# Sequence product of an FNet-SwiGLU kernel: split right sides stored once and reloaded in the last two sets, and no split of the a21 block by itself

## The chip, the core and the metric

The kernel runs on one core of a Trainium2 chip. The metric is the device time of one execution in microseconds (us). The engines named below are PE (TensorE, the matrix multiplier), ACT (ScalarE), DVE (VectorE), POOL (GpSimd) and SP (SyncE). Every engine works through its own list of instructions in order. Transfers between HBM and the on-chip memory (SBUF) are issued by SP, which fills the queue that the profile calls q1, and by POOL, which fills q0. Both queues are served by the same 16 DMA engines.

## What is computed

```python
xn = layernorm(x)                                   # x: 2048 x 640
a, b = xn @ hid_re.T, xn @ hid_im.T                 # hid: 640 x 640
s = seq_re @ a - seq_im @ b                         # seq: 2048 x 2048
g = silu((silu(xn @ w_gate) * (xn @ w_up)) @ w_down)   # F = 1536
out = x + s * g
```

All of it is in 32-bit floats.

## The kernel before

**Numbers in two parts.** A matrix product of 32-bit floats is made of three matmuls on rounded operands. `split` (L184) turns an operand into a high part, a rounded copy made by ACT (L192), and a low part, the operand minus the high part, made by DVE (L197, or L199 with a factor). `mm3` (L210) multiplies high by high, high by low and low by high (L213, L214, L215) into one PSUM bank. A PSUM bank is 128 x 512; there are 8. Split operands live in an SBUF arena called `hl`, everything else in an arena called `raw`.

**Stages.** The program runs four *sets* of the sequence product (`seq(0)` to `seq(3)`), and then, twice, the hidden product (`hid`), the gate and up products (`gate_up`) and the down product (`down`).

**A set.** Set k multiplies blocks of the sequence matrix (real part for even k, imaginary for odd k; two of the four column chunks of 512 per set) by xn. It is a 2 x 2 block product in Strassen's manner: left blocks a11, a12, a21, a22 of the sequence matrix, right blocks b11 to b22 of xn, and seven products p1 to p7 in place of eight. The last 128 of the 640 columns of xn do not take part in this; their two halves, d1 and d2, are multiplied directly: a11 d1 + a12 d2 into bank 6, a21 d1 + a22 d2 into bank 7. Each left block comes in four pieces g = 0 to 3 of 128 x 1024 floats (512 KB). A piece is loaded by SP (L575, in `load`), or added onto a buffer in SBUF by an accumulating transfer that POOL issues (L580, in `accumulate`), or added by DVE (L583, in `add`). `operand` (L586) splits a piece, and `right_operand` (L592) splits the right side of a product, or the sum of right sides that it needs (`right`, L467). The right sides are the same in all four sets and are split again in each.

In set 0 the kernel opens with p1 of sets 0 and 1 side by side (`opening`, L668; the second one's result is put aside as `ahead["s1"]` and `ahead["d1"]`, copied out of PSUM by L241). Then comes a phase `d`, that splits a21 and multiplies it by d1 (L741), then p5 with the left side a21 + a22, which is made by accumulating a22 onto the same buffer after the split of a21, then p2, p6, p3, p7, p4. In the other sets the order is p1 (not in set 1), d, p2, p5, p6, p3, p7, p4. `down` uses the same order through `strassen` (L251).

**Later stages.** `down_operands` (L506) makes the split right sides of `down`, from w_down, and stores them to `d_dram`; `down` reloads them (L1021). It is a generator, and `gate_up` of the first half advances it twice for each of its middle ten column blocks.

**What sets the order.** All instructions are written into a `Plan` with a planned time on PE's clock, at 0.226 us for each matmul. `prod(lead, ...)` plans an instruction `lead` us before the product that needs it, `post(..., after=)` some us after the product that it follows. The instructions are sorted by planned time, and each engine's list is that order. `place` gives every buffer its offset in an arena from the planned lifetimes. On the chip nothing waits for the planned time: an instruction runs when its engine has done the one before it and its data and buffers are free.

Of the kernel before, what the change touches and what calls it, by code (L numbers as in the profile page):

```python
# [7 lines left out]
F32 = mybir.dt.float32  # L8
# [15 lines left out]
HL_KB, RAW_KB = 95, 111  # L24
# [113 lines left out]
def tile_fnet_swiglu(  # L138
# [112 lines left out]
    def strassen(tag, groups, get, top, dop, result, end=False):  # L251
# [73 lines left out]
        def a21(g):  # L325
            X[g] = get(21, g)
            return operand("d", g, X[g])

# [4 lines left out]
        def s_1(g):  # L333
            V[g] = get(22, g)
# [22 lines left out]
        phase("d", None, a21, (2, 1))  # L357
# [3 lines left out]
        phase("p5", b3, s_1)  # L361
# [15 lines left out]
        if not end:  # L377
            run("p4", ops["p4"], None, None, None, (2, 2))
# [4 lines left out]
        dw, dkeys = dop(2)  # L383
# [80 lines left out]
    p_dram = dram.tile([2, NC, ND, P, TC], F32, name="p_dram")  # L464
    sums = {}

    def right(p, g, lead):  # L467
# [6 lines left out]
        def new(what, a, b, op):  # L474
            if (what, g) not in sums:
                name = pl.buf((what, g), "raw", 1024)
                view = lambda a=0, n=4: raw(name).rearrange("p (a b) -> p a b", b=256)[:, a:a + n]
# [16 lines left out]
        if p == "p7":  # L494
# [4 lines left out]
            return a  # L499
        return quad(int(p[1]) - 1, 2, P)  # L500


    d_names = ("p1", "p2", "d1", "d2", "p3", "p5", "p6", "p7", "p4")
    d_dram = {(p, g): dram.tile([P, 768 if p[0] == "d" else 1536], F32, name=f"d_{p}_{g}") for g in range(2) for p in d_names}

    def down_operands():  # L506

        for g in range(2):
# [10 lines left out]
            for p in d_names:  # L519
                b11, b12, b21, b22 = (quad(*q) for q in ((0, 0), (0, 1), (1, 0), (1, 1)))  # L520
                made = {"p5": (b11, b12, ALU.subtract), "p6": (b11, b22, ALU.add),
                        "p7": (b12, b22, ALU.subtract), "p4": (b21, b11, ALU.subtract)}
# [32 lines left out]
    def seq(k):  # L555
# [36 lines left out]
        def right_operand(p, g, per):  # L592

            width = P if p[0] == "d" else 256
            sums, high, low = LEAD.get(("T" + p, per * g), LEAD.get("T" + p, LEAD["T"])) if fresh else LEAD["T"]
# [8 lines left out]
            for i in range(per):  # L604
                top[p, per * g + i] = name, sub, (sub + i) * width

# [4 lines left out]
        def run(*parts, order=None):  # L611
# [6 lines left out]
            for i, g in order or [(0, g) for g in range(4)]:  # L618
                p, left, banks, direct = parts[i]
# [3 lines left out]
                s = left(g)  # L623
                for kk in (2 * g, 2 * g + 1):
# [41 lines left out]
        Y, R = {}, {}  # L666

        def opening():  # L668
# [42 lines left out]
            for kk in range(8):  # L711
                for i, banks, db in part:
# [15 lines left out]
            evict(ahead["s1"], b1, after=1)  # L728
            evict(ahead["d1"], (b3[0],), after=1)
# [405 lines left out]
```

## Time and profile before

| | |
|---|---|
| time, median of 3 runs | 993.39 us (992.28 to 993.47) |
| profiled execution: its own time / its span | 993.8 us / 991.7 us |
| mean granted TensorE clock | 0.995 |
| PE busy | 979.3 us, 4300 matmuls |
| DVE busy / ACT busy / POOL busy | 717.2 / 497.8 / 106.4 us |
| bytes moved by DMA | 182.18 MB, mean 184 GB/s |

The span runs from the first to the last instruction; the execution's own time has 2.1 us more around it. A busy PE includes matmuls that overlap in its pipeline, so PE's time is read from the spacing of its matmuls. The view of windows gives, for a stretch of the span, the busy time of each engine with the number of instructions, the granted clock, the busy share of the 16 DMA engines and the rate in GB/s.

### The profile page before, as it was taken

The page shows a single profiled execution, that of the slowest core. Times are in us where ns is not written, and L with a number is a line of the kernel's source. Part 1 is how long each engine was busy: PE and PEld are TensorE (multiplying, and loading weights), DVE is VectorE, ACT ScalarE, POOL GpSimd, SP SyncE. Part 2 cuts the span into 40 slices and gives each one's busy share as a digit, 9 for nine tenths or more (in the row PEclk, how much of TensorE's full clock was granted, in tenths as well). Part 3 has the DMA queues.
Part 4 walks back from the last instruction along what each step waited for, and adds up shares of the span by engine and source line. Part 5 has one row for each costly group of instructions (what it writes and reads, how often), then busy time and mean ns, then how long its engine had stood idle before and what let it go on. Part 6 is the DMA issues. An engine that isn't in the chain of part 4 may idle for free.

```text
span 991.7 us, 11754 instructions
## 1 busy us (share of the span) xinstructions
PE 979.3 (99%) x4300; PEld 804.7 (81%) x4300; DVE 717.2 (72%) x942; ACT 497.8 (50%) x716; POOL 106.4 (11%) x175
## 2 busy tenths in 40 slices
PE   9989999999999999999999999999999999999998
PEld 5778888788888888888888888888888888888886
DVE  6889867965875595377678787687568666666685
ACT  5585652755455554424655555444334544445342
POOL 0380111011101010000111110000010100000000
PEclk9989999999999999999999999999999999999999
DMA  9788687575757493842645344679860211105683
GB/s 337 208 210 227 223 217 180 171 237 135 180 191 222 108 264 116 288 163 107 250 191 181 138 165 164 211 264 354 293 230 28 89 45 53 54 27 191 219 290 127
DMA packets 72185, 182.18 MB, mean 184 GB/s; under 512 B 6528, under 2 KB 22144, under 8 KB 72128
## 3 DMA queue, kind: packets, MB, share of 16 engines
q1 hardware_dynamic: 57792, 127.81, 38.0%
q0 software_dynamic: 14336, 53.63, 19.6%
q8 instruction: 33, 0.54, 0.2%
q14 instruction: 24, 0.20, 0.1%
HBM read 147.85 MB, written 33.57 MB: 183 GB/s over the span
## 4 chain that ended last, share of the span: by engine, by line
PE 91%; DMA 3%; DVE 2%; ACT 2%; issue 1%; SPq 0%; POOL 0%; DVEq 0%; ACTq 0%
PE ps L214 30%; PE ps L213 30%; PE ps L215 30%; DMA raw<-in_cs 3%; DVE hl L197 1%; ACT hl L192 1%; DMA p_dram<-raw 1%; ACT raw L454 0%; DVE raw L583 0%; DVE bst L421 0%; ACT raw L241 0%; POOL raw L580 0%; DVE raw L246 0%; SPq L686 0%; SPq L412 0%
## 5 line engine op out<-in xcount | busy, mean ns | idle before, releaser
L213 PE MATMUL ps<-hl 128*128 128x512 f32 (+1 forms) x1424 | 554.6, 389 | 5.3 <-ACT raw L241 5.3
L214 PE MATMUL ps<-hl 128*128 128x512 f32 (+1 forms) x1424 | 554.0, 389 | 0.1
L215 PE MATMUL ps<-hl 128*128 128x512 f32 (+1 forms) x1424 | 553.6, 389 | 0.0
L192 ACT ACTIVATE hl<-raw 128x1024 fp32r<-128x1024 f32 (+7 forms) x509 | 374.5, 782 | 284.4 <-PE ps L215 54.1
L197 DVE TENSOR_TENSOR hl<-raw,hl 128x1024 fp32r<-128x1024 f32 (+5 forms) x438 | 394.7, 931 | 121.8 <-ACT hl L192 76.9
L213 PEld LDWEIGHTS ps<-hl 128*128 128x128 f32 x1424 | 268.0, 188 | 62.5 <-ACT raw L241 6.1
L214 PEld LDWEIGHTS ps<-hl 128*128 128x128 f32 x1424 | 267.9, 188 | 56.2 <-DVE hl L197 0.7
L215 PEld LDWEIGHTS ps<-hl 128*128 128x128 f32 x1424 | 267.9, 188 | 55.2
L241 ACT ACTIVATE raw<-ps 128x512 f32<-128x512 f32 (+1 forms) x120 | 78.0, 670 | 106.6 <-PE ps L215 80.9
L246 DVE TENSOR_TENSOR raw<-ps,raw 128x512 f32<-128x512 f32 (+1 forms) x93 | 74.6, 803 | 54.1 <-PE ps L215 52.4
L1005 DVE TENSOR_TENSOR raw<-raw 128x512 f32<-128x512 f32 x24 | 16.6, 692 | 50.1 <-ACT raw L1004 50.0
L918 DVE TENSOR_TENSOR raw<-raw 128x256 f32<-128x256 f32 (+1 forms) x96 | 47.7, 518 | 0.0
L580 POOL DMA_DIRECT2D raw<-in_cs x36 | 32.3, 953 | 140.3 <-DVE raw L583 81.0
L199 DVE SCALAR_TENSOR_TENSOR hl<-raw,hl 128x384 fp32r<-128x384 f32 (+4 forms) x71 | 41.2, 580 | 7.3 <-PE ps L215 2.9
L583 DVE TENSOR_TENSOR raw<-raw 128x1024 f32<-128x1024 f32 x28 | 34.1, 1219 | 10.8 <-DMA raw<-in_cs 10.7
L1067 POOL DMA_DIRECT2D out<-raw x10 | 6.7, 671 | 302.1 <-DMA hl<-d_p 175.1
L657 POOL DMA_DIRECT2D p_dram<-raw x24 | 17.5, 772 | 198.1 <-DVE raw L246 163.4
L871 DVE TENSOR_TENSOR raw<-raw 128x1024 f32<-128x1024 f32 (+1 forms) x24 | 23.9, 1040 | 6.8 <-DMA raw<-in_xt 4.7
L983 ACT ACTIVATE raw<-raw 128x512 f32<-128x512 f32 x24 | 15.2, 632 | 22.1 <-DVE raw L246 22.1
L843 POOL DMA_DIRECT2D y_dram<-raw x20 | 10.8, 546 | 132.5 <-ACT raw L241 132.5
L1004 ACT ACTIVATE raw<-ps 128x512 f32<-128x512 f32 x24 | 14.3, 594 | 21.0 <-PE ps L215 21.0
L533 POOL DMA_DIRECT2D d_p<-hl x28 | 15.1, 541 | 79.7 <-ACT hl L192 65.6
(49 smaller groups left out, 191.6 us busy)
## 6 DMA issues: line engine op xcount, KB each, us to landing
raw<-in_cs SPq DMA_DIRECT2D x82, 512.0 KB, 6.1
hl<-d_p SPq DMA_DIRECT2D x56, 384.0 KB, 4.4
raw<-in_cs POOLq DMA_DIRECT2D x36, 512.0 KB, 8.9
raw<-in_wb SPq DMA_DIRECT2D x24, 640.0 KB, 4.5
d_p<-hl POOLq DMA_DIRECT2D x28, 384.0 KB, 2.9
raw<-p_dram SPq DMA_DIRECT2D x8, 1280.0 KB, 11.1
p_dram<-raw POOLq DMA_DIRECT2D x16, 512.0 KB, 7.5
raw<-in_hd SPq DMA_DIRECT2D x20, 320.0 KB, 8.1
```

The source lines that it names most:

```text
L192: nc.scalar.activation(like(hl(dst, 0, a, n)), src(), AF.Copy, scale=1.0 if scale is None else scale)
L197: nc.vector.tensor_tensor(lo, src(), hi, op=ALU.subtract)
L199: nc.vector.scalar_tensor_tensor(lo, src(), scale, hi, op0=ALU.mult, op1=ALU.subtract)
L213: nc.tensor.matmul(o, w(0), m(0), start=first, stop=False, skip_group_check=True)
L214: nc.tensor.matmul(o, w(0), m(1), start=False, stop=False, skip_group_check=True)
L215: nc.tensor.matmul(o, w(1), m(0), start=False, stop=True, skip_group_check=True)
L241: pl.post(lambda: nc.scalar.activation(wide(raw(dst, a, n)), pair(b), AF.Copy), pkeys(b), [(dst, a)], after)
L246: pl.post(lambda: nc.vector.tensor_tensor(wide(raw(dst, a, n)), pair(b), wide(raw(other)), op=op), [*pkeys(b), (other, 0)], [(dst, a)], after)
L580: pl.prod(lead, lambda: nc.gpsimd.dma_start(wide(raw(name)), source(q, g), accum_op=ALU.add), [], [(name, 0), (name, 1)], 8)
L583: pl.prod(lead, lambda: nc.vector.tensor_tensor(raw(dst), raw(dst), raw(src), op=ALU.add), [(src, 0)], [(dst, 0)])
L871: pl.prod(46 - 6 * q - 2 * i - half, lambda i=i, op=op, part=part, rows=rows, nb=nb: nc.vector.tensor_tensor(part(), part(), raw(rows, i * ...
L918: pl.prod(lead, lambda o=o, a=a, b=b, op=op: nc.vector.tensor_tensor(o(), a(), b(), op=op), [(w, 0)], [(c, lead)])
```

## The change

Matrix sizes, the number of matmuls and the order of later stages stay. The change has these parts:

- Phase `d` is gone, in the sets and in `strassen`. The left side of p5, a21 + a22, is also multiplied by d1 into bank 7, and in the end a22 is multiplied by a new right side d3 = d2 - d1 instead of d2. So a21 is not split by itself. In sets 0 and 1 the a22 pieces are accumulated straight after the load of a21.
- The split right sides are stored to HBM (`t_dram`) by POOL: those of p6, p3, p7, d3 and p4 in set 0, those of p1, p2, d1, d2 and p5 in set 1, where p1's are split for this alone. In sets 2 and 3 `right_operand` reloads them with two SP transfers for each half and splits nothing.
- In sets 2 and 3 each of the four left blocks is loaded once, and kept; the sums are made by DVE in place of accumulating transfers.
- `down_operands` (with d3 as a tenth right side) is advanced in sets 2 and 3, ten times in each, and not in `gate_up`.
- In set 0 the rows 1024 to 2047 of x are loaded by SP, planned earlier (before: six of the eight loads by POOL); the pieces of p5 come in plain order; the last step of the opening does the second product first, and the copies of its results are planned earlier.
- The `hl` arena has 94 KB in each partition instead of 95, the `raw` arena 112 instead of 111.

The core of the diff:

```diff
-        phase("d", None, a21, (2, 1))
         phase("p2", b1, a12, (1, 2))
...
-        phase("p5", b3, s_1)
+        phase("p5", b3, s_1, (2, 1))
...
+    t_names = ("p1", "p2", "d1", "d2", "d3", "p3", "p5", "p6", "p7", "p4")
+    t_dram = {(p, q): dram.tile([P, 2 * (512 if p[0] == "d" else 1024)], F32, name=f"t_{p}_{q}") for p in t_names for q in (0, 1)}
...
+        if p == "d3":
+            return new("nt5", quad(1, 2, P), quad(0, 2, P), ALU.subtract, P)
...
         def right_operand(p, g, per):
 
             width = P if p[0] == "d" else 256
+            if k > 1:
+                n = 4 * width
+                name = pl.buf(("T", k, p, g), "hl", 2 * n)
+                for i in range(2):
+                    pl.prod(18, lambda i=i: nc.sync.dma_start(
+                        hl(name, i).bitcast(F32), t_dram[p, g][:, i * n:i * n + n]), [("td", p, g)], [(name, "hl"[i], 0)])
+                for i in range(4):
+                    top[p, 4 * g + i] = name, 0, i * width
+                return
...
+            if (shared if p in ("p1", "p2", "d1", "d2", "p5") else fresh):
+                n = 4 * width
+                for i in range(2):
+                    pl.prod(low - 2, lambda i=i: nc.gpsimd.dma_start(
+                        t_dram[p, g][:, i * n:i * n + n], hl(name, i).bitcast(F32)), [(name, "hl"[i], 0)], [("td", p, g)], 6)
...
+                if k > 1 and (g == 1 or g == 3 and p in ("p2", "p6")):
+                    next(spare, None)
...
-                for i, banks, db in part:
+                for i, banks, db in part if kk < 7 else part[::-1]:
...
-            evict(ahead["s1"], b1, after=1)
-            evict(ahead["d1"], (b3[0],), after=1)
+            evict(ahead["d1"], (b3[0],), after=-1.5)
+            evict(ahead["s1"], b1, after=-1)
...
         def p5(g):
+            if k > 1:
+                R[g], V[g] = load(21, g, 26), load(22, g, 26)
+                add(Y[g], R[g], 14)
+                add(R[g], V[g], 12.5)
+                return operand("p5", g, R[g])
+            R[g] = load(21, g, 26 if fresh else 22)
+            accumulate(R[g], 22, g, 18 if fresh else 16)
             s = operand("p5", g, R[g])
             if fresh:
-                accumulate(R[g], 11, g, LEAD["p5", g][1] - 0.1)
+                accumulate(R[g], 11, g, LEAD["p5"][1] - 0.1)
             return s
 
-        def d(g):
-            R[g] = load(21, g, 26 if fresh else 18)
-            s = operand("d", g, R[g])
-            accumulate(R[g], 22, g, LEAD["d"][1] - 0.1 if fresh else 7.5)
-            return s
-
         def p2(g):
+            if k > 1:
+                Z[g] = load(12, g, 24)
+                return operand("p2", g, Z[g])
             if fresh:
                 for kk in (8 + 2 * g, 9 + 2 * g):
-                    load_x(kk, (32, 27.5, 25.4, 29.4)[g], nc.gpsimd if g else nc.sync)
+                    load_x(kk, 40 + 2 * g, nc.sync)
...
         def p6(g):
+            if k > 1:
+                pl.prod(12, lambda: nc.vector.tensor_tensor(raw(R[g]), raw(Y[g]), raw(V[g]), op=ALU.add),
+                        [(Y[g], 0), (V[g], 0)], [(R[g], 0)])
+                return operand("p6", g, R[g])
...
+        if shared:
+            for q in (0, 1):
+                right_operand("p1", q, 4)
         s1 = ahead["s1"] if shared else copy("s1", b2)
-        run(("d", d, (), (2, 1)))
...
-        run(("p4", p4, (), (2, 2)))
+        run(("p4", p4, (), (2, 3)))
...
-            if j == 0 and f and f != NF - 1:
-                next(spare, None)
```

How the engines' lists move is shown at two places. The first is ACT's list at the end of the opening, in set 0. L192 makes high parts, L454 (L449 after) applies the layer norm, and L241 copies PSUM out: 128x512 is `ahead["d1"]`, the two of 128x1024 are `ahead["s1"]` and set 0's own p1. Before:

```order
L192 ACTIVATE hl_65<-raw_66 128x128
L192 ACTIVATE hl_65<-raw_66 128x1024 x6
L241 ACTIVATE raw_66<-ps_67 128x1024
L241 ACTIVATE raw_66<-ps_67 128x512
L241 ACTIVATE raw_66<-ps_67 128x1024
L192 ACTIVATE hl_65<-raw_66 128x1024 x2
L454 ACTIVATE raw_66<-raw_66,sm_69,rowst_72 128x640 x2
```

After:

```order
L192 ACTIVATE hl_65<-raw_66 128x128
L192 ACTIVATE hl_65<-raw_66 128x1024
L241 ACTIVATE raw_66<-ps_67 128x512
L192 ACTIVATE hl_65<-raw_66 128x1024
L241 ACTIVATE raw_66<-ps_67 128x1024
L192 ACTIVATE hl_65<-raw_66 128x1024
L241 ACTIVATE raw_66<-ps_67 128x1024
L192 ACTIVATE hl_65<-raw_66 128x1024
```

The copy of `ahead["d1"]`, which frees the bank in which p5 begins, stood second of the three copies, behind six splits, the last of them that of p5's second piece in its old order (g = 2). Now it stands first of the copies, and the split just ahead of it is that of p5's piece 1.

The second place is POOL's list at the start of set 1. `p_dram` takes results of a set, L580 (L579 after) are the accumulating transfers, and `t_p1_0` and the like are the stored right sides (the name, then the half, then a running number). The x2 is the high and the low part. Before:

```order
L657 DMA p_dram_74<-raw_66 128x2x512 x2
L580 DMA raw_66<-in_cs 128x1024 x2
L657 DMA p_dram_74<-raw_66 128x512
L580 DMA raw_66<-in_cs 128x1024 x2
L852 DMA mr_dram_73<-rowst_72 32x32 x4
L657 DMA p_dram_74<-raw_66 128x2x512
```

After:

```order
L617 DMA t_p1_0_75<-hl_65 128x1024 x2
L617 DMA t_p1_1_76<-hl_65 128x1024 x2
L617 DMA t_p2_0_77<-hl_65 128x1024 x2
L617 DMA t_d2_0_81<-hl_65 128x512 x2
L672 DMA p_dram_74<-raw_66 128x512
L617 DMA t_p2_1_78<-hl_65 128x1024 x2
L617 DMA t_d2_1_82<-hl_65 128x512 x2
L579 DMA raw_66<-in_cs 128x1024
L877 DMA mr_dram_73<-rowst_72 32x32 x4
L579 DMA raw_66<-in_cs 128x1024
L672 DMA p_dram_74<-raw_66 128x2x512
L617 DMA t_p5_0_87<-hl_65 128x1024 x2
```

Eight stores of 512 KB and four of 256 KB now stand ahead of the first accumulating transfer of set 1, and those of p5's right side stand between the second and the third.

More of the change, by code (lines that the diff above doesn't have):

```diff
@@ L23 @@
 MM = 0.226
-HL_KB, RAW_KB = 95, 111
+HL_KB, RAW_KB = 94, 112
 class Plan:
@@ L763, in p3 @@
         def p3(g):
-            add(R[g], load(12, g, 17), 12)
+            add(R[g], Z[g] if k > 1 else load(12, g, 17), 12)
             return operand("p3", g, R[g])
@@ L797, in p4 @@
         def p4(g):
-            last.append(operand("p4", g, load(22, g, 17)))
+            last.append(operand("p4", g, V[g] if k > 1 else load(22, g, 17)))
             return last[-1]
-        run(("p4", p4, (), (2, 2)))
+        run(("p4", p4, (), (2, 3)))
         result("d2", (dbank[2],), None, None)
```

36 lines of the change are left out of this document (16 added, 20 removed), and 3 rows, old and new, of the table LEAD.

## The prediction

> **What bounds the kernel now.** I read the page first, then the waits of PE, the chain of waits around the longest, and the view of windows by stage.
>
> ```profile
> span 991.7 us, 11754 instructions
> PE 979.3 (99%) x4300; PEld 804.7 (81%) x4300; DVE 717.2 (72%) x942; ACT 497.8 (50%) x716; POOL 106.4 (11%) x175
> ...
> PE ps L213 <- ACT raw L241: 5.3, 2, 5.0
> ```
>
> PE decides nearly everywhere. It waits for another engine for some 5 us, nearly all in one place. The windows show where; the columns are the stretch, its length, the busy time of PE, weight loads, DVE, ACT and POOL with their instructions, the granted clock, the DMA share and GB/s.
>
> ```profile
> core 0: us, PE busy (x) PEld busy (x) DVE busy (x) ACT busy (x) POOL busy (x), PEclk, DMA share, GB/s
> 41.60:47.30 5.70, 5.64 (x25) 4.32 (x23) 4.67 (x7) 2.98 (x3) 0.91 (x2) 1.00 1.02 234
> 47.30:52.30 5.00, 0.01 (x1) 0.02 (x1) 2.22 (x5) 2.52 (x4) 4.52 (x10) 0.84 1.07 212
> 52.30:57.60 5.30, 5.30 (x13) 4.15 (x14) 5.23 (x10) 5.30 (x7) 4.49 (x6) 0.51 1.04 332
> 57.60:132.30 74.70, 74.70 (x331) 61.86 (x330) 66.43 (x75) 48.91 (x59) 23.46 (x42) 1.00 0.80 215
> 174.30:214.00 39.70, 39.44 (x173) 31.96 (x172) 31.91 (x30) 25.17 (x28) 2.02 (x3) 1.00 0.63 210
> 214.00:312.00 98.00, 98.00 (x434) 81.16 (x433) 70.03 (x63) 51.14 (x55) 11.06 (x14) 1.00 0.65 184
> 312.00:410.00 98.00, 98.00 (x434) 81.16 (x433) 66.68 (x62) 51.04 (x57) 11.00 (x14) 1.00 0.64 179
> ```
>
> Undisturbed, 331 matmuls take 74.70 us, which is 0.2257 us for one. The change keeps their number, so it can only win where this spacing is broken. That is at the end of the opening: 5.0 us without a matmul, then 13 matmuls at a granted clock of 0.51 in 5.3 us instead of 2.9, which is 2.4 us more. In the second half of set 1, 173 matmuls would take 39.05 us and took 39.70. The sets 2 and 3 (the rows from 214 and from 312) are at the pace. All that can be won is 5.0 + 2.4 + 0.65 = 8.05 us. The chain of waits shows what the 5.0 us waited for, and the timeline why it came so late.
>
> ```profile
> 39.50 10.25 DMA raw<-in_cs
> 49.76 0.02 issue
> 49.78 1.06 ACT hl L192
> 50.83 1.41 ACT raw L241 x2
> 52.24 0.04 issue
> 52.28 0.79 PE ps L213
> ...
> 36.72 1.06 POOL L580 DMA_DIRECT2D raw<-in_cs  x1 [35.39 <-DVE hl L197]
> ```
>
> PE waits for ACT's copy of `ahead["d1"]` out of the bank in which p5 starts; the copy stands behind the split of a p5 piece, and that waits for an accumulating transfer. POOL could not issue the first of these before 36.72 us, because the low split of a21 still had to read the buffer.
>
> **The opening (set 0).** In the changed kernel no split of a21 reads the buffer, so the transfer waits only for the load of the piece. These rows are of SP's loads of whole pieces, and of transfers by size in the first 30 us.
>
> ```profile
> L575 SPq DMA_DIRECT2D raw<-in_cs x76: 327/328/1546, 15.3 to 365.2; - x76
> ...
> raw<-in_cs SPq DMA_DIRECT2D x13, 512.0 KB, 8.9
> ...
> 9.00:29.00 20.00, 20.00 (x81) 14.69 (x80) 16.16 (x43) 12.91 (x24) 0.00 (x0) 1.00 1.03 408
> 666.00:686.00 20.00, 20.00 (x90) 16.56 (x89) 15.61 (x11) 8.11 (x7) 0.71 (x1) 1.00 1.06 364
> ```
>
> The first load of a21 is issued at 15.3 us and lands some 8.9 us later, at 24.2. Behind it SP still has to bring three pieces and, newly ahead of them, eight row blocks of x: 1.6 + 2.6 = 4.2 MB, at 408 GB/s 10.3 us. Accumulating costs more: while 47.30 to 52.30 held little else, all engines were busy at 212 GB/s, so 0.524 MB take 2.5 us and four pieces 9.9 us. The last accumulated piece is there at 24.2 + 20.2 = 44.4 us; PE needs it, if p5 begins at 41.6 and a piece is 18 matmuls (4.06 us), at 53.8, less some 4 us for landing and split. Piece 1, whose split is the last ahead of the copy in ACT's new order, is there by about 34 us, and the opening's second product, now done first, ends 9 matmuls before 41.6, at 39.6. The copy then has 2 us to run beside the other product. So the wait and the slow clock go, 5.0 + 2.4 = 7.4 us, with a margin of some 4 us. If that cover fails, up to 7.4 us come back.
>
> **Set 1: the stores.** This is the price of the change in the first half. POOL's list has 8 stores of 512 KB and 4 of 256 KB (5.24 MB) and 0.26 MB of results ahead of the first accumulating transfer. The stores are planned 9 us before set 1 begins, and p5 begins 72 matmuls, 16.3 us, after that. Loads of that stretch, six pieces or 3.1 MB, share the engines. These rows price the rest.
>
> ```profile
> L197 DVE TENSOR_TENSOR hl<-raw,hl 128x1024 fp32r<-128x1024 f32 x186 | 220.4, 1220 | 61.8 <-ACT hl L192 38.6 <-PE ps L214 11.8 <-PE ps L215 11.3
> L192 ACT ACTIVATE hl<-raw 128x1024 fp32r<-128x1024 f32 x190 | 191.8, 1052 | 126.7 <-PE ps L214 37.2 <-PE ps L215 34.1 <-DVE raw L885 14.0
> ...
> raw<-in_cs SPq DMA_DIRECT2D x21, 512.0 KB, 5.7
> raw<-in_cs POOLq DMA_DIRECT2D x8, 512.0 KB, 8.5
> ```
>
> Upper end: everything in turn at 408 GB/s. 8.6 MB are 21.2 us, the accumulation 2.5, so -9 + 23.7 = 14.7 us after the set's begin; with 2 us to land and 2.3 for the split (1.05 + 1.22), p5's first operand comes at 19.0, 2.7 us late. The third piece has 2.1 MB of stores and results, 1.6 MB of loads (9.0 us) and two more accumulations (5.0) before it: 14.7 + 14.0 + 4.3 = 33.0, due at 16.3 + 8.1 = 24.4, so 8.6 us late. Then the clock falls as at 52.30, 2.4 us more: 11.0. Lower end: SP's loads are planned 17 to 22 us ahead and land in 5.7, so they may all be through before. Without them the first operand comes at 11.3 and the third at 21.4, both in time: 0. I take the middle, half of the loads in the stretch: the third piece at 27.2, 2.8 us late, and half of the slow clock, 1.2, because no row shows a wait of that length. That is +4.0. The waiting instruction is ACT's split of a p5 piece; behind it on ACT stand the second half of p5's right side and the later pieces, for which p5 alone waits. The 0.65 us of before sit in the same set behind the same kind of transfer; I count half of it won, 0.3.
>
> The Trainium skill, "TensorE: Matmul & The Clock Gate", Part 1, says that the clock falls after an idle window of about 3.4 us, and rises after as long a busy one. The 5.0 us wait with 0.51 behind it agrees; by that rule a wait of 2.8 us alone would cost no clock, and the sum would be 1.2 us lower.
>
> **Sets 2 and 3: the reloads.** Each set takes 98 us. It used to move 18 MB. Now it loads seven right sides and three narrow ones (28 x 0.524 + 12 x 0.262 = 17.8 MB), 16 pieces (8.4), w_down (2.0), and stores w_down's operands (14 x 0.393 + 6 x 0.197 = 6.7) and results (2.6): 37.5 MB or 383 GB/s. That fits below 408, the rate of 20 us of such loads, and not below 364, that of 20 us with short rows among them. Within a set it is uneven: all pieces and the first three right sides fall into the first half, some 23.5 MB or 480 GB/s, so at 408 a backlog of 3.5 MB, 8.6 us, builds up. Right sides are planned 18 us ahead, pieces 26, of which DVE and ACT need 4.7 (two additions, one split); the second half, at 286 GB/s, works it off. So PE waits nowhere at 408; I take +0.4 for both sets, the ends being 0 and the rival's 10. What is queued behind a late load on SP is every later load; PE and DVE's additions wait for it. The price rests on rows of loads, since no window of before mixes stores and loads at this rate.
>
> **What costs nothing.** These rows have the sizes that are still missing.
>
> ```profile
> L197 DVE TENSOR_TENSOR hl<-raw,hl 128x512 fp32r<-128x512 f32 x62 | 42.6, 687 | 21.3 <-ACT hl L192 9.6 <-PE ps L214 8.1 <-PE ps L215 2.0
> L197 DVE TENSOR_TENSOR hl<-raw,hl 128x384 fp32r<-128x384 f32 x52 | 28.5, 551 | 0.6 <-ACT hl L192 0.6
> L197 DVE TENSOR_TENSOR hl<-raw,hl 128x768 fp32r<-128x768 f32 x12 | 11.5, 955 | 3.8 <-ACT hl L192 3.8
> L525 DVE TENSOR_TENSOR raw<-raw 128x768 f32<-128x768 f32 x8 | 7.6, 951 | 0.0
> ```
>
> DVE in sets 2 and 3 loses 14 + 4 right-side splits (14 x 1.22 + 4 x 0.69 = 19.8) and four of a21 (4.9), and gains eight additions (9.8) and w_down's ten operands (7 x 0.955 + 3 x 0.55 for the low parts, 4 x 0.951 + 0.55 for the sums, 12.7), so its 70.03 us in 98 stay; ACT only loses. Taking w_down's work out of gate and up wins nothing, because PE is full there, as in the down product, where d3's reload (4 x 0.2 MB, planned 14 us ahead) is hidden in a DMA share of 0.79:
>
> ```profile
> 478.00:618.00 140.00, 140.00 (x617) 115.25 (x617) 107.32 (x203) 80.34 (x160) 22.14 (x41) 1.00 0.49 178
> 618.00:691.00 73.00, 73.00 (x324) 60.45 (x323) 55.96 (x40) 30.67 (x27) 2.00 (x3) 1.00 0.79 267
> ```
>
> **The sum.** The profiled execution took 993.8 us, 2.1 more than its span and 0.4 more than the median of the runs, 993.4. 993.8 - 7.4 - 0.3 + 4.0 + 0.4 = 990.5, against the median 990.1.
>
> **Rivals.** First, *the DMA engines bound sets 2 and 3*. It decides once the mixed stream stays under the 383 GB/s that PE's pace asks for. For it speak the 364 above and that loads can only be issued when PE frees a right side's buffer, so the queue is not always full; against it the 408, held for 20 us. At 364 a set takes 37.5 MB / 364 GB/s = 103 us, 5 us more; two sets give 10, so 1000.1 us: slower. The Trainium skill, "DMA: Bandwidth & Descriptors", Specifications, gives an HBM limit of about 358 GB/s for a core; by it a set would take 104.8 us and the time would be 990.1 - 0.4 + 13.6 = 1003.3. The trace's 408 speaks against that limit for a core alone.
>
> Second, *the accumulating transfers of set 1 come as late as the upper end says*: 990.1 + 7.0 = 997.1, slower. For it: before, such a transfer took up to 10.25 us to land with nothing but its own kind around. Against it: the loads run ahead.
>
> Third, *the opening's wait stays*, because SP's eight blocks of x now delay the pieces: 990.1 + 7.4 = 997.5. Against it is the margin of 4 us.
>
> **How the numbers follow.** My forecast, with set 1's cost anywhere from 0 to 5.5 us, has 0.50 and its own range is 985 to 991.6. The bound sets 2 and 3 have 0.24, set 1's upper end 0.19, the opening's wait 0.07. The range runs from all won and nothing paid, 993.4 - 8.05 = 985.3, rounded to 985, to the two slower rivals together, 990.1 + 7.0 + 10 = 1007. A difference of 0.2%, 2 us, is about what can be told from no change here. Faster is the forecast without its last margin, 0.47; within 0.2% lies that margin, and the milder outcomes of set 1 and the opening, 0.14; slower 0.39.
>
> **What would show it.** Right: no gap in PE's matmuls between 41 and 58 us and the clock at 1.0; in set 1 a wait of p5 for ACT's split behind an accumulating transfer, 2 to 4 us; in sets 2 and 3 a DMA rate near 380 GB/s with PE at 0.2257 us for a matmul. Wrong: PE waits there for transfers of the stored right sides, or for DVE's additions behind loads of pieces, or a DMA share of 1 with a lower rate; or the copy of `ahead["d1"]` still ends a wait at the opening's end.

## Result, and the profile after

| | before | after |
|---|---|---|
| median of the runs | 992.88 us (992.28 to 993.47) | 1003.89 us (1002.49 to 1006.45) |
| span of the profiled execution | 991.7 us | 1004.6 us |
| its granted clock | 0.995 | 0.993 |

The changed kernel is slower: the ratio is 1.0114, with a 95% interval of 1.0092 to 1.0136. The prediction had 990.1 us. The page of the changed kernel, its totals, the rows of the clock and of the DMA engines over the span, and POOL's queue (packets, MB, share of 16 engines):

```profile
span 1004.6 us, 11893 instructions
PE 983.5 (98%) x4300; PEld 806.6 (80%) x4300; DVE 682.4 (68%) x914; ACT 452.8 (45%) x668; POOL 112.3 (11%) x197
...
PEclk9999997999999999999999999999999999999999
DMA  9969999989989998993220112669950320104793
...
q0 software_dynamic: 16800, 61.89, 18.5%
```

PE still bounds the kernel and DVE and ACT have less to do, as intended. But a slice of the DMA row is 25 us: from the fourth slice to the seventeenth, 75 to 427 us, the 16 engines now stay at 8 or 9 tenths. The same row of the kernel before:

```profile
DMA  9788687575757493842645344679860211105683
```

What PE waited for between 50 and 200 us (us in total, times, longest):

```profile
PE ps L213 <- ACT hl L192: 9.5, 3, 6.4
PE ps L214 <- DVE hl L197: 3.9, 4, 1.9
PE ps L213 <- DVE raw L246: 0.9, 1, 0.9
```

These are waits for split left pieces (L192, L197) and for a subtraction that frees a PSUM bank (L246). The windows of the changed kernel at the places that the prediction named:

```profile
core 0: us, PE busy (x) PEld busy (x) DVE busy (x) ACT busy (x) POOL busy (x), PEclk, DMA share, GB/s
40.00:50.00 10.00, 10.00 (x46) 8.26 (x45) 4.25 (x9) 4.44 (x5) 4.13 (x11) 1.00 1.06 251
92.80:96.50 3.70, 1.79 (x8) 1.12 (x7) 3.66 (x4) 2.50 (x3) 0.53 (x1) 0.97 1.04 423
96.50:99.50 3.00, 3.00 (x9) 2.33 (x8) 3.00 (x3) 2.24 (x3) 0.53 (x1) 0.50 1.03 347
146.50:155.00 8.50, 1.61 (x4) 0.70 (x3) 1.23 (x1) 1.06 (x1) 4.52 (x8) 0.76 1.05 268
155.00:158.00 3.00, 3.00 (x9) 2.30 (x9) 1.86 (x2) 2.52 (x3) 1.74 (x3) 0.55 1.04 425
168.60:171.50 2.90, 2.90 (x8) 2.22 (x8) 2.09 (x3) 1.94 (x2) 0.00 (x0) 0.53 1.01 410
220.00:260.00 40.00, 40.00 (x179) 33.10 (x178) 20.16 (x19) 12.46 (x13) 3.45 (x6) 1.00 1.03 412
320.00:360.00 40.00, 40.00 (x176) 32.64 (x176) 17.45 (x16) 11.75 (x13) 3.46 (x6) 1.00 1.03 410
```

The opening's stall is gone (first row: 46 matmuls in 10 us). A small wait is left at 55 us, where PE loses 1.7 us: the last piece of p5's left side got its accumulating transfer at 40.65 us, which landed at 53.71, and ACT could not split it before:

```profile
53.79 1.06 ACT L192 ACTIVATE hl<-raw 128x1024 fp32r<-128x1024 f32 x1 [4.79 <-DMA raw<-in_cs]
```

The large new stall is in set 1 (146.50: four matmuls in 8.5 us), with the slow clock behind it, a second one 17 us later (its slow clock is the row of 168.60), and a smaller one in set 0 at 92.80. Sets 2 and 3 run at PE's pace; in these two stretches of 40 us the engines move 412 and 410 GB/s. The chain of waits ahead of set 1's first stall (start, us, what):

```profile
127.01 12.49 DMA t_p<-hl
139.50 0.29 issue
139.78 12.42 DMA raw<-in_cs
...
154.34 11.35 DMA raw<-in_cs
```

A store of a right side, and after it the accumulating transfers of p5, each with 11 to 12 us from issue to landing. p5 does not need what that store moves. But POOL never has more than eight transfers under way in these traces: each uses the semaphore of the one eight places before it in the list, and is issued only after that one has landed. All 17 transfers that POOL issued from 127 to 153 us in the changed kernel followed such a landing within 0.6 us; in the kernel before, 2 of 8 did. So the first accumulating transfer of p5 could not even be issued before 139.78 us, when the store of 127.01 had landed.

To compare kernels I add up, from the starts of PE's matmuls in each trace, by how much each spacing exceeds 0.227 us (where by over 0.08 us). This is the time that PE lost, by stage. The cold start, 4.2 to 5.4 us in every kernel, is left out. The wait at 55 us counts to the rest of set 0. The kernels other than the first two are those of the next section. One of the seven executions of the last row but one took 1659.43 us at a granted clock of 0.556, and its ratio further down leaves that one out.

| us lost | opening | rest of set 0 | set 1 | sets 2, 3 | later | median us |
|---|---|---|---|---|---|---|
| before | 7.9 | 0 | 0.8 | 0 | 0.3 | 992.88 |
| after | 0 | 6.7 | 14.6 | 0.3 | 0 | 1003.89 |
| stores by SP | 0 | 12.0 | 12.3 | 1.7 | 0 | 1010.54 |
| p1 stored late | 0 | 7.4 | 8.8 | 0 | 0 | 1000.56 |
| stores behind | 0 | 5.2 | 13.3 | 1.3 | 0 | 1005.19 |
| a22 added by DVE | 0 | 6.0 | 5.5 | 1.4 | 0 | 997.94 |
| set 0's stores only | 0 | 7.5 | 0 | 5.4 | 0 | 998.15 |
| set 1's stores only | 0.2 | 3.5 | 8.6 | 1.7 | 0 | 999.84 |
| w_down stored twice | 0.1 | 6.9 | 12.3 | 15.6 | 0.8 | 1019.21 |
| no stores | 0 | 4.5 | 1.5 | 0 | 5.7 | 996.06 |
| the same, p3 accumulated | 0.5 | 3.0 | 0 | 0 | 11.0 | 995.74 |
| d3 in the sequence only | 0 | 1.8 | 1.0 | 0 | 1.7 | 990.03 |
| the same, p3 accumulated | 0 | 2.4 | 1.9 | 0 | 1.7 | 991.33 |
| the same, sums by POOL | 0 | 4.8 | 1.6 | 0 | 1.7 | 992.62 |

From before to after that is -7.9 + 6.7 + 13.8 + 0.3 - 0.3 = 12.6, and 0.5 more at the cold start, against 12.9 between the spans.

### The profile page after: what moved, and what is told of

Read it like the earlier page. It is cut to its first block, busy times and chain, and to the rows that moved or that the text cites. A ratio compares the mean times of both kernels' runs of the same rounds, so it can differ in the third digit from the quotient of the medians.

```text
span 1004.6 us, 11893 instructions
## 1 busy us (share of the span) xinstructions
PE 983.5 (98%) x4300; PEld 806.6 (80%) x4300; DVE 682.4 (68%) x914; ACT 452.8 (45%) x668; POOL 112.3 (11%) x197
## 4 chain that ended last, share of the span: by engine, by line
PE 83%; DMA 6%; issue 4%; DVE 3%; POOL 2%; ACT 1%; SPq 0%; POOLq 0%; ACTq 0%; DVEq 0%
PE ps L214 28%; PE ps L215 28%; PE ps L213 28%; DMA raw<-in_cs 4%; DMA t_p<-hl 2%; DVE hl L197 1%; ACT hl L192 1%; DVE bst L416 1%; POOL t_p L617 1%; ACT raw L449 0%; POOL t_d L617 0%; SPq L407 0%; POOL raw L579 0%; SPq L701 0%; DVE mv L418 0%
## 5 line engine op out<-in xcount | busy, mean ns | idle before, releaser
L192 ACT ACTIVATE hl<-raw 128x256 fp32r<-128x256 f32 (+7 forms) x461 | 329.0, 753 | 355.8 <-DVE raw L943 57.2
L197 DVE TENSOR_TENSOR hl<-raw,hl 128x1024 fp32r<-128x1024 f32 (+6 forms) x392 | 340.3, 893 | 150.9 <-ACT hl L192 102.6
L241 ACT ACTIVATE raw<-ps 128x512 f32<-128x512 f32 (+1 forms) x120 | 78.5, 669 | 92.3 <-PE ps L215 91.2
L246 DVE TENSOR_TENSOR raw<-ps,raw 128x512 f32<-128x512 f32 (+1 forms) x93 | 74.6, 804 | 51.3 <-PE ps L215 50.9
L582 DVE TENSOR_TENSOR raw<-raw 128x1024 f32<-128x1024 f32 x36 | 43.9, 1220 | 15.2 <-DMA raw<-in_cs 14.7
L199 DVE SCALAR_TENSOR_TENSOR hl<-raw,hl 128x256 fp32r<-128x256 f32 (+4 forms) x69 | 38.6, 561 | 15.2 <-ACT hl L192 8.5
L579 POOL DMA_DIRECT2D raw<-in_cs x20 | 18.6, 998 | 59.5 <-DMA raw<-in_cs 35.6
L533 POOL DMA_DIRECT2D d_p<-hl x28 | 15.3, 547 | 65.2 <-ACT hl L192 36.8
```

The source lines that it names most:

```text
L192: nc.scalar.activation(like(hl(dst, 0, a, n)), src(), AF.Copy, scale=1.0 if scale is None else scale)
L197: nc.vector.tensor_tensor(lo, src(), hi, op=ALU.subtract)
L199: nc.vector.scalar_tensor_tensor(lo, src(), scale, hi, op0=ALU.mult, op1=ALU.subtract)
L241: pl.post(lambda: nc.scalar.activation(wide(raw(dst, a, n)), pair(b), AF.Copy), pkeys(b), [(dst, a)], after)
L246: pl.post(lambda: nc.vector.tensor_tensor(wide(raw(dst, a, n)), pair(b), wide(raw(other)), op=op), [*pkeys(b), (other, 0)], [(dst, a)], after)
L579: pl.prod(lead, lambda: nc.gpsimd.dma_start(wide(raw(name)), source(q, g), accum_op=ALU.add), [], [(name, 0), (name, 1)], 8)
```

## Experiments

**The stores in another queue, or later in the same.** The first theory was one of order: on POOL, p5's accumulating transfers stand behind the stores. The rival was bandwidth: the 16 engines serve both queues and are full, whatever stands first.

```diff
-                    pl.prod(low - 2, lambda i=i: nc.gpsimd.dma_start(
+                    pl.prod(low - 2, lambda i=i: nc.sync.dma_start(
                         t_dram[p, g][:, i * n:i * n + n], ...
```

> The changed kernel, with the stores of the right sides issued by SP instead of POOL. In the changed kernel PE loses 14.6 us in set 1 (p5 waits twice for ACT's split behind an accumulating transfer) and 6.7 us in set 0. Theory 'queue order' (the accumulating transfers are late because they stand behind the stores in POOL's queue, while the engines could serve them): set 1's loss falls below 5 us and the time to about 994. Theory 'bandwidth' (the 16 DMA engines are full in sets 0 and 1, in whichever queue the stores stand): set 1 still loses 10 us or more, now perhaps behind late loads of pieces, and the time stays at 1000 to 1008.

Measured: 1010.54 us (1009.51 to 1011.23), ratio to before 1.0176 (1.0161 to 1.0191), 6.6 us more than the change as it is and above both ranges; set 1 still lost 12.3 us. On SP the loads stand behind the stores, so this alone did not separate the theories. The next one does: POOL keeps the stores, but set 1's are planned 24 us later.

```diff
-                    pl.prod(low - 2, lambda i=i: nc.gpsimd.dma_start(
+                    pl.prod(low - 2 - (0 if fresh else 24), lambda i=i: nc.gpsimd.dma_start(
```

> As the changed kernel, but set 1's stores are planned 24 us later, so that on POOL the four accumulating transfers of p5 stand ahead of all of them (in the changed kernel stores of 4.2 MB stand ahead of the first and 2.6 MB more among them); as many bytes as before in set 1. Queue-order theory (p5's accumulating transfers are late because they stand behind the stores): set 1's loss falls from 14.6 us to under 6, the rest being set 0's stores that are still under way: 993 to 997 us. Bandwidth theory (16 DMA engines that are full pass an accumulating transfer on no sooner, or the stores then hold up p6's): set 1 still loses 10 us or more, 1000 to 1005 us.

Measured: 1005.19 us (1004.37 to 1007.08). The four transfers of p5 were now issued at 123.9, 128.9, 132.0 and 134.9 us; in the changed kernel they were issued at 139.8, 146.8, 154.3 and 154.9. PE's waits for p5 were gone. These are its waits from 50 to 220 us in this run, and then its chain of waits before the longest of them:

```profile
PE ps L214 <- DVE hl L197: 11.2, 4, 8.1
PE ps L213 <- DVE raw L246: 2.6, 1, 2.6
```

```profile
170.28 14.44 DMA t_p<-hl
184.72 0.01 issue
184.73 1.23 DVE hl L197
185.96 0.04 issue
186.00 0.79 PE ps L214
```

The wait moved from p5 to p3, where the low part of a left piece now waited for the landing of a store, 14.4 us after its issue: it needs the place in `hl` that the store still reads, and the plan keeps such a place for 6 us only. Set 1 lost 13.3 us and not 14.6. So p5's waits hung on the order in POOL's queue, as the first theory said, but taking them away did not take the loss away, as the rival said. The engines were near full in both kernels: their share from 120 to 180 us was 0.97 in the changed kernel and 1.04 here. The windows from 60 to 180 us of the kernel before, of the changed kernel and of this run:

```profile
60.00:180.00 120.00, 119.74 (x528) 98.44 (x527) 97.25 (x98) 69.35 (x78) 27.34 (x42) 1.00 0.74 200
```

```profile
60.00:180.00 120.00, 106.94 (x445) 86.13 (x444) 82.52 (x87) 59.71 (x68) 46.66 (x78) 0.94 0.93 312
```

```profile
60.00:180.00 120.00, 112.15 (x489) 90.89 (x487) 90.35 (x90) 63.15 (x71) 46.34 (x74) 1.00 0.97 321
```

The engines were busy 0.74 of the time before. The 26% that were free are 31 us. The stores are 28 x 0.524 + 12 x 0.262 = 17.8 MB, which at the 408 GB/s of the prediction's loads are an estimated 43.6 us of all engines: 12 us too many for that stretch, in which all of them were issued (69.6 to 160.7 us).

**Fewer bytes in sets 0 and 1.** Four runs take bytes or engine time away, or move them to a later time. In the first, p1's right sides, which set 1 splits only to store them, come after p6 (`u2` is p6's result there).

```diff
-        if shared:
-            for q in (0, 1):
-                right_operand("p1", q, 4)
...
+            for q in (0, 1):
+                right_operand("p1", q, 4)
             u2 = pl.buf(("u2", k), "raw", 2 * TC)
```

> As the changed kernel, but the right side p1 (2.1 MB of stores) is split and stored in set 1 behind p6's operands and not ahead of the set. Stores theory: ahead of p5's accumulating transfers stand then 3.1 MB of stores and not 5.2, by 400 GB/s 5.2 us less, so p5's first wait of 6.6 us in set 1 shrinks to 1 to 3 us: 994 to 999 us. Rival (the accumulating transfers are slow by themselves, 12 us each beside loads, whatever stands ahead): set 1 keeps its 14 us, 1002 to 1005 us.

Measured: 1000.56 us (1000.18 to 1001.53); set 1 lost 8.8 us. The first wait of p5 is gone and that of its third piece (3.8 us) is left. The time lies between the two ranges. Set 1 stores as many bytes as before, only 2.1 MB of them later, and lost 5.8 us less; so the order counts too, unlike in the run with all stores behind, and why the two runs differ stays open. In the second, a22 is not accumulated in set 1 but loaded and added by DVE.

```diff
-            accumulate(R[g], 22, g, 18 if fresh else 16)
+            if fresh:
+                accumulate(R[g], 22, g, 18)
+            else:
+                add(R[g], load(22, g, 20), 12.5)
```

> The changed kernel, with a22 of set 1 loaded by SP into buffers of its own and added by DVE, instead of accumulated by POOL; the stores stay where they are. Theory 'queue order': p5 of set 1 no longer depends on POOL's queue, so its two waits (9.2 and 5.4 us with the slow clock) go, and the time falls to 990 to 994. Theory 'bandwidth': four transfers cost 1.3 us of the engines instead of 2.5, 5 us less, but loads now wait beside the stores; the time falls by 2 to 6 us, to 998 to 1002.

Measured: 997.94 us (996.54 to 998.77), ratio 1.005 (1.0033 to 1.0067). Set 1 lost 5.5 us. By the rate of the prediction's 5.0 us stall (212 GB/s) an accumulated piece occupies the engines for 2.5 us, a loaded one at 408 GB/s for 1.3, so four pieces take 4.8 us less; that much the loss fell, and 4.2 more. p5's two waits are gone, as the queue-order theory had it, but the time fell by 5.95 us, the most that the bandwidth theory had, and not to 994. What is left is one wait of 3.9 us at 177 us with the slow clock behind it. In the third and fourth, only one of the two sets stores. In the third it is set 0; the other right sides are split again in sets 2 and 3, whose left pieces are loaded and accumulated as in the kernel before.

```diff
-            if k > 1:
+            if k > 1 and p not in ("p1", "p2", "d1", "d2", "p5"):
                 n = 4 * width
...
-            if (shared if p in ("p1", "p2", "d1", "d2", "p5") else fresh):
+            if fresh and p not in ("p1", "p2", "d1", "d2", "p5"):
```

> Only the right sides stored in set 0 (p6, p3, p7, d3, p4) are stored and reloaded; p1, p2, d1, d2 and p5 are split again in sets 2 and 3, whose left blocks are loaded and accumulated as before. Set 1 has no stores then. Both theories: set 1's 14.6 us go, to less than 2; set 0's 6.7 us stay within 2 us, as its stores do. Time 990 to 993. If set 1 still loses over 5 us, its loss is not from its stores, and if set 0 loses under 3 us, that loss was not from its stores.

Measured: 998.15 us (997.45 to 999.82), where I had expected 993 at most. Set 1, with all its accumulating transfers, lost nothing; so those are not late by themselves. Set 0 lost 7.5 us. The 5.4 us in sets 2 and 3 are new: accumulating transfers are there again, with five right sides reloaded beside them. PE waits at 377 us behind a transfer of a left piece that took 17.07 us, from 357 to 374 us, where the DMA share was 1.04 at 311 GB/s.

In the fourth it is set 1, and sets 2 and 3 reload its tiles in place of set 0's, so that as many bytes move there but the numbers are not those of the product.

```diff
+                src = {"p3": "p1", "p6": "p2", "p7": "p5", "p4": "p1", "d3": "d1"}.get(p, p)
...
-            if (shared if p in ("p1", "p2", "d1", "d2", "p5") else fresh):
+            if shared and p in ("p1", "p2", "d1", "d2", "p5"):
```

> As the changed kernel, but set 0 stores nothing (9.4 MB less between 70 and 125 us); sets 2 and 3 reload as many bytes, only from tiles that set 1 stored, so their numbers are those of other right sides. Theory that set 1's loss is made by what stands in set 1 itself, its 8.4 MB of stores beside its accumulating transfers: set 1 still loses 12 to 15 us, and set 0 some 4 us at 112 us as in the run without stores: 1000 to 1003 us. Rival (set 0's stores keep the 16 DMA engines full up to 125 us, and set 1 starts with their backlog): set 1 loses under 7 us, 991 to 996 us.

Measured: 999.84 us (998.85 to 1001.0). Set 1 lost 8.6 us, between the two theories: of its 14.6 us some 6 are gone with set 0's stores, and the rest comes from set 1 itself. Set 0's stores alone cost set 1 nothing in the run above, so these 6 us arise only where both sets store.

**No stores at all.** Every set splits its own right sides, the left pieces of sets 2 and 3 and w_down's operands are made as before; the opening and d3 stay. Its buffers do not fit into arenas of 94 and 112 KB; here, and in the kernels built on this one, the arenas have 93 and 113.

```diff
-            if k > 1:
+            if False:
                 n = 4 * width
...
-            if (shared if p in ("p1", "p2", "d1", "d2", "p5") else fresh):
+            if False:
                 n = 4 * width
...
-                if k > 1 and (g == 1 or g == 3 and p in ("p2", "p6")):
-                    next(spare, None)
...
+            if j == 0 and f and f != NF - 1:
+                next(spare, None)
```

> No right side of the sequence product is stored; every set splits its own, as in the kernel before; w_down's operands are made in gate and up again, the left pieces of sets 2 and 3 are loaded and accumulated as before. What stays of the change is the right side d3, by which a21 needs no split of its own, and the order of the opening. (Arenas of 93 and 113 KB.) Stores theory: both the 6.7 us that the changed kernel lost in set 0 and the 14.6 us of set 1 come from the 512 KB stores, so nearly all of them goes, and what the opening won (some 7 us) is left: 985 to 988.5 us, faster than both kernels. Rival (set 0's loss is that of the loads moved there, the x blocks and the accumulating transfer queued last): set 0 keeps some 6 us and only set 1's goes: 989.5 to 993 us, no faster than before or hardly.

Measured: 996.06 us (993.91 to 997.19), ratio 1.0028 (1.0018 to 1.0038). Both theories missed. Set 1's loss went as expected, but 4.5 us stayed in set 0, at another place, and gate and up lost 5.7 us that the changed kernel had not lost. In set 0 the timeline of DVE shows it:

```profile
105.80 4.62 DVE L197 TENSOR_TENSOR hl<-raw,hl 128x1024 fp32r<-128x1024 f32 x4
110.34 1.22 DVE L475 TENSOR_TENSOR raw<-raw 128x1024 f32<-128x1024 f32 x1
112.77 1.23 DVE L197 TENSOR_TENSOR hl<-raw,hl 128x1024 fp32r<-128x1024 f32 x1 [1.21 <-ACT hl L192]
113.91 1.22 DVE L246 TENSOR_TENSOR raw<-ps,raw 128x1024 f32<-128x1024 f32 x1
```

PE needs the subtraction L246 at 112.5 us, and it ends at 115.1. In the kernel before, the same operation ended at 116.4, and PE came there at 120.1: PE is 7.6 us earlier now and DVE only 1.3. I read this as the opening's stall having been time in which DVE caught up; part of the opening's gain is then given back here. But 1.21 us of the wait are DVE's own wait for ACT's high part, one operation ahead of the subtraction (third line), so the place of the subtraction in DVE's list may be as much to blame. The loss in gate and up has its longest wait at 617 us; the chain there:

```profile
611.41 3.15 DMA d_p<-hl
614.56 3.08 issue
617.64 1.48 ACT hl L192
619.13 0.49 ACT raw L241
```

ACT's split waits behind the store of one of w_down's operands, of which d3 makes ten in place of nine. (In the trace this store lands at 617.57 us; the view shows the second half of its time as issue.) So the next run, built on this one, keeps d3 in the sequence product and gives the down product its own split of a21 back.

```diff
+        phase("d", None, a21, (2, 1))
...
-        phase("p5", b3, s_1, (2, 1))
+        phase("p5", b3, s_1)
...
-    d_names = ("p1", "p2", "d1", "d2", "d3", "p3", "p5", "p6", "p7", "p4")
+    d_names = ("p1", "p2", "d1", "d2", "p3", "p5", "p6", "p7", "p4")
```

> As the run without stores (996.06 us), but the down product has its own split of a21 again and no d3, so w_down has nine operands and not ten to be made, stored and reloaded; d3 is left in the sequence product alone. Theory that the run without stores lost 5.8 us in gate and up because w_down's ten operands are made there (PE waits at 549, 611 and 617 us, the last 2.9 us behind a store of such an operand): 990 to 991.5 us. Rival (these waits come from the arenas' places, 93 and 113 KB, which this kernel has too): 995 to 997 us.

Measured: 990.03 us (988.49 to 992.21), ratio 0.9973 (0.9963 to 0.9983): 0.3% faster than the kernel before. The loss in gate, up and down fell from 5.7 to 1.7 us, with the same arenas, so the rival, that the places in the arenas cause it, fell.

**The wait at 112 us.** Two edits were tried to take work off DVE before it. With the first, p3's pieces of a12 are added by accumulating transfers (four additions of 1.22 us less), once on the run without stores and once on the better one.

```diff
-            add(R[g], Z[g] if k > 1 else load(12, g, 17), 12)
+            if fresh:
+                accumulate(R[g], 12, g, 15)
+            else:
+                add(R[g], load(12, g, 17), 12)
```

> As the run without stores (996.06 us), but in set 0 the pieces of a12 that p3 needs are added by accumulating transfers and not by DVE, four additions of 1.22 us less. Theory that DVE is behind in set 0 once the opening's stall is gone (it was busy 90% and more from 60 to 110 us, and PE waited 2.7 us at 112 us for its subtraction, with 1.6 us of slow clock behind): that wait goes, 990.5 to 993 us. Rival (the wait is one of DVE's order, the subtraction standing behind one split that waits for ACT, however busy DVE was before): 995 to 997 us.

> The two edits together: p3's additions by accumulating transfers in set 0, and d3 in the sequence product alone. If both theories hold, the opening's gain of some 7 us is left nearly whole: 984.5 to 987.5 us, faster than both kernels. If only one does: 990 to 993 us.

Measured: 995.74 us (994.35 to 998.64) and 991.33 us (ratio 0.9977, 0.9966 to 0.9988), no better than without it: PE still lost 3.0 and 2.4 us in set 0. DVE had its free time too early: in the second run it was busy for 13.2 of the 20 us from 70 to 90 us, in place of 18.4, and for 19.9 of the next 20 in both. The rival of the first of these runs, the place of the subtraction in DVE's list, was not tested and stays open. The first of the two also lost 11.0 us in gate, up and down, where its instructions are those of the run without stores, which lost 5.7 there; why it is more stays open. With the other edit, on the better run, the four sums for the right sides p4 and d3 go to POOL.

```diff
-                pl.prod(lead, lambda: nc.vector.tensor_tensor(view(), a[0](), b[0](), op=op), ...
+                eng = nc.gpsimd if what in ("nt4", "nt5") else nc.vector
+                pl.prod(lead, lambda: eng.tensor_tensor(view(), a[0](), b[0](), op=op), ...
```

> As the run with d3 in the sequence product alone (990.03 us), but the four sums for the right sides p4 and d3 in set 0 (two of 1.22 us, two of 0.69 us on DVE) are made by POOL, which has little to do there. Theory that DVE is short of time from 84 to 114 us, 28 operations in a row: the subtraction for which PE waits at 112 us comes some 3 to 4 us earlier, that wait (2.4 us, and 0.9 us of slow clock behind it) goes: 986 to 988 us. Rival (POOL takes several us for such a sum, or slows DVE down while it runs, so that the split behind it comes as late): 990 to 993 us.

Measured: 992.62 us (990.22 to 994.03). The rival was right. The groups of DVE's splits of 1024 columns from 84 to 112 us, first in the run with d3 in the sequence only, then here, and POOL's four sums here, which ran from 84 to 112 us too (busy, mean ns):

```profile
L197 DVE TENSOR_TENSOR hl<-raw,hl 128x1024 fp32r<-128x1024 f32 x15 | 17.8, 1221 | 0.1
```

```profile
L197 DVE TENSOR_TENSOR hl<-raw,hl 128x1024 fp32r<-128x1024 f32 x13 | 18.7, 1474 | 0.0
...
L481 POOL TENSOR_TENSOR raw<-raw 128x1024 f32<-128x1024 f32 x2 | 5.7, 2866 | 8.1 <-DVE hl L197 8.1
L481 POOL TENSOR_TENSOR raw<-raw 128x512 f32<-128x512 f32 x2 | 3.5, 1750 | 4.6 <-DVE raw L587 4.6
```

A sum takes POOL 2.87 us where DVE needs 1.22, and DVE's own operations slow down beside it, from 1.22 to 1.47 us in the mean. The Trainium skill, "GPSIMD Engine Reference", 1. Specifications, says that POOL shares its SBUF interfaces with VectorE, in contention with VectorE's instructions of two SBUF inputs; these rows agree.

**How much room sets 2 and 3 have.** Every store of w_down's operands is made a second time, to a place that nobody reads.

```diff
+                    pl.prod(-4, lambda p=p, g=g, dst=dst, i=i, n=n: nc.gpsimd.dma_start(
+                        e_dram[p, g][:, i * n:i * n + n], hl(dst, i).bitcast(F32)),
+                        [(dst, "hl"[i], 0)], [], 6)
```

> As the changed kernel, but every store of w_down's operands in sets 2 and 3 is made twice, the second time to a place that nobody reads: 6.7 MB more in each set, 44 MB in 98 us or 450 GB/s. Bound at some 410 GB/s (the rate that the changed kernel held for 40 us at a stretch): a set takes about 107 us where PE must wait for the reloads, so 5 to 9 us more in each, 1013 to 1022 us. If the changed kernel's sets 2 and 3 still have room in the DMA engines (rates above 430 GB/s possible, or only stores late that nobody waits for): 1003 to 1008 us.

Measured: 1019.21 us (1015.9 to 1020.6), 15.3 us more than the changed kernel; PE lost 15.6 us in sets 2 and 3. Its two largest groups of waits from 235 to 460 us, and the window of 340 to 360:

```profile
PE ps L213 <- DMA hl<-t_p: 4.7, 1, 4.7
PE ps L214 <- DVE hl L197: 1.9, 1, 1.9
```

```profile
340.00:360.00 20.00, 14.05 (x42) 9.97 (x43) 6.35 (x6) 5.86 (x7) 3.24 (x6) 0.74 1.03 412
```

PE's pace asks for an estimated 450 GB/s here (44 MB in 98 us); the engines give 412 in this stretch, and PE waits for the reloads. In the changed kernel, where the pace asks for 383, it did not.

## Why the prediction was wrong, step by step

**The opening, -7.4:** right in the main. The 7.9 us of waits and slow clock behind the copy of `ahead["d1"]` are gone in every run with the new opening, within 0.5 us, and the rival that they stay fell. But the margin of 4 us was not there: the last accumulated piece landed at 53.71 us, where the sum had 44.4, and PE lost 1.7 us at 55 us, inside the stretch of 41 to 58 us in which no gap was to be. The loads ahead of it took until 40.4 us in place of 34.5, and four loads of a12 and two accumulations of a11, which the sum did not count, were issued from 34.9 to 41.2 us and shared the engines. In the run without stores that transfer landed at 51.2 us, beside three loads of a12, and nothing was lost there; no store had been issued by then in either kernel. The step also left out what is late next: the subtraction by DVE at 112 us in set 0. Without any store set 0 loses 1.8 to 4.8 us.

**Set 1's stores, +4.0:** this step failed. The loss is 14.6 us against 0.8 before, above even the upper end of 11.0. I took the middle between loads that are through and loads that are not; the engines were full in any case (a share of 1.05 at the stall), so the lower end did not exist. And I had POOL issue the accumulation at will and sized it by its own engine time, 2.5 us. In the trace POOL's list itself was held up: the first transfer was issued only at 139.78 us, when the store eight places before it had landed, and it took 12.42 us more, behind everything that both queues held. It landed 21.8 us after the set's beginning (130.4 us), where the upper end had 14.7. So p5's first operand came 7.6 us late (6.58 for the high part, 1.03 for the low) where the upper end had 2.7, and the third piece added another 2.80 + 1.03. The slow clock came twice. That the stores cost it is shown by the runs in which set 1 stores nothing, where it lost 0 to 1.9 us. How much of it is the engines' rate and how much the order in POOL's list is not separated: p5 off that list, or p1's stores later, took 9 and 5.8 us of the loss away, all stores later only 1.3.

**Set 0's stores:** never priced. I added up bytes for sets 2 and 3, where the rate was just enough, and not for sets 0 and 1, where 17.8 MB met engines that were already busy 74% of the time. The row was on the page and in the windows (a DMA share of 0.80 from 57.6 to 132.3 us). Set 0's part is 9.4 MB. Of the 6.7 us lost there, the 3.8 us at 92.8 are a wait for p3's pieces and the clock behind it, which is 0.1 us without stores; 1.7 us are the wait at 55 us, before any store, and 1.1 us one for the subtraction at 119 us. And some 6 us of set 1's loss go when set 0 stores nothing.

**The 0.65 of set 1, half won:** not to be told from this kernel, whose set 1 loses 14.6 us. In the runs without stores in that set it loses from 0 to 1.9 us, and 1.0 in the best one.

**Sets 2 and 3, +0.4:** right, 0.3 measured. The choice of 408 over 364 GB/s held: 412 and 410 over 40 us each, with stores and loads mixed. The first rival, with this place as the bound, fell, and so did its price by a limit of 358 GB/s. The Trainium skill, "HBM Reference", Specifications (TRN2), says itself that a core streaming alone reaches about 425 GB/s and that 358 is its share when both cores of a pair stream; the trace is near the first.

**What costs nothing:** right for DVE and ACT in sets 2 and 3 and for the down product. The move of w_down's operands was worth something after all, since d3 makes one more: with all ten in gate and up, 5.7 us were lost there, and none in the changed kernel.

**The clock:** I had quoted the Trainium skill's "TensorE: Matmul & The Clock Gate", Part 1, that the clock falls after an idle window of some 3.4 us. The row of 96.50 shows 0.50 behind a wait of only 2.1 us, which differs from that rule. Waits of 2.7 us (stores by SP, at 122 us) and 2.5 us (set 1's stores only, at 113 us) had no slow clock behind them. So a wait of 2 to 3 us may or may not cost it.

The second rival, set 1's upper end, named the right place and the right late transfer at 997.1 us, and was still too low by the parts above. The sum with the measured terms: 993.8 - 7.9 + 13.8 + 6.7 + 0.3 - 0.3 + 0.5 = 1006.9, against 1006.45 for the profiled execution.

## What to carry to other kernels

Before transfers are added to a stage, add up its bytes and set their engine time against the idle share of the DMA engines there, in every stage that stores or loads and not only in the one that profits; beyond that share, another queue made the loss larger here, and a later place for all stores moved the wait and hardly shortened it. An operand that ACT and DVE make in time anyway is not worth storing: here PE was at its pace in sets 2 and 3 already, so the stores could only cost, and the best version keeps none of them. Where a list has many transfers, look at what holds up the issue of an urgent one, and not only at its bytes. When a stall is removed, look up which other engine had been catching up during it.

## What was not expected of the hardware

With the 16 DMA engines near full, POOL's transfers of 512 KB took 7 to 16 us from issue to landing (those issued from 120 to 155 us in the changed kernel), against an estimated 1.3 us (a plain one, at 408 GB/s) or 2.5 us (an accumulating one, at 212 GB/s) of engine time. POOL's list had at most eight transfers under way, so such a time also sets when the next one is issued. Four sums on POOL, 9.2 us in all, slowed DVE's splits of 1024 columns by a fifth over the 28 us in which they lay. And a wait of 2.1 us was followed by half the clock in one place, while one of 2.7 us in another was not.
